# The two layers of an MLP alternate by threes: one chunk of the first layer, then one token block of the second

## The chip, the cores and the metric

The kernel runs on one core of one Trainium2 chip. The metric is the device time of one launch in microseconds, as the median of several runs. For the kernel before, the median of three runs is 957.42 us (957.02 to 958.61). Beside these stands one profiled execution. The TensorE (PE) does the matrix products and the transposes, VectorE (DVE) and ScalarE (ACT) read their results out of PSUM, GpSimd (POOL) works on SBUF alone, and SyncE (SP) starts all the transfers.

## The reference

The reference is a windowed attention followed by a two-layer MLP, in float32.

```python
# q, k, v: (batch 8, heads 8, 576, 64)
scores = scale * np.matmul(q, k.transpose(0, 1, 3, 2))
# heads 0-3: the last 32 keys; heads 4-7: every 4th of the last 128 keys
scores = np.where(masks[None, :, :, :], scores, -1000000000.0)
attn = softmax(scores)                       # written out in the original
x = (attn @ v).transpose(0, 2, 1, 3).reshape(4608, 512)
h = x @ w_in                                 # 512 -> 2048
g = np.where(h >= 1, h, np.where(h <= -1, 0.0, (h + 1) ** 2 / 4))
out = g @ w_out                              # 2048 -> 512
```

## The kernel before

**Attention.** A head is worked on in six query tiles of 96 rows, each against 128 keys. Scores go to PSUM (tag `att`, two banks), DVE adds the mask and takes the minimum for the softmax (lines 169 and 240), ACT takes the exponentials (L246), DVE and POOL normalise (L260, L263, L264), DVE transposes (L286; for the first 16 heads TensorE does, L310), TensorE multiplies with the values (L344), and `store_x` splits the result into a rounded part `xh` (ACT, L328) and a rest `xl` (DVE, L329). These are the tokens of the MLP, kept in SBUF.

**MLP.** The 4608 tokens are nine tiles of 512 (`t`), and the 2048 hidden units are sixteen blocks of 128 (`f`). A step is one pair (t, f), so there are 144 steps, f inside t. Every product is made of three in the fast float32 format: high by high, low by high, high by low.

- `layer1(t, f)`: one PSUM bank `h` (tag `h`, two banks) gets 12 matmuls of 128x512, that is four chunks `c` of the 512 inputs with three terms each (L382). Then come five operations on it, here called the chain: DVE clamps h into `y` (L396), ACT squares it (L399), DVE takes the maximum back into the bank (L401), ACT rounds it to `gh` (L402), DVE stores the rest `gl` (L405). `gh` and `gl` have two buffers each.
- `layer2(t, f)`: for each of four token blocks `m` of 128, three matmuls of 128x512 accumulate onto bank `acc0` to `acc3` (L418). After f = 15 each `acc` is copied out by ACT (L430) or DVE (L428) and stored from there (L431). So these four banks, the two of `h` and the two of `att` are the eight banks of PSUM.

**Order.** The instructions of TensorE and SP stand exactly in the order in which the program writes them; those of DVE, ACT and POOL are put in order when the program is built, by a simulated time line with priorities. The chain is raised by 60 places, the score reductions of later heads by 100. The second layer runs two steps behind the first (`lag = 2`). The work of attention hangs on slots: `run(u)` issues what is placed on slot u, and a step s has two of them, `run(2 * s)` and `run(2 * s + 1)`. From head 16 on, slots go in fours: three successive slots hold the scores of two query tiles each (the third also the split of the next head's q and k, the loads and the softmax), and every second time the fourth holds the products with the values. The three lie on slots 2s + 1 of an odd step and 2s and 2s + 1 of the even step after it, the values on slot 2s of an odd step. The DVE transposes of a head are written down with the first scores of the head after it. The last slot is in step 111; after it the steps consist of the MLP alone.

**The weights.** Each of the 32 weight tiles arrives as float64 and is turned into two tiles by ACT, DVE and POOL (L115 to L132). `behind(marks, ...)` puts that work on ACT and DVE after the chain of a given step: in step s the tile `wo` s and the tile `wi` s+3 come after the chain of step s-2.

**Start.** Half of the first layer of steps 0 and 1 (chunks 0 and 1) is done before the loop. The loop's steps 0 and 1 add chunks 2 and 3 to them. Slots 0 and 1 hold the TensorE transposes of heads 8 and 9, slot 2 their values, slots 3 and 4 the scores of heads 10 and 11.

Of the kernel before, what the change touches and what calls it, by code (L numbers as in the profile page):

```python
# [35 lines left out]
TOK = 512  # L36
NT = B * S // TOK
NF = DF // 128
NC = DM // 128
# [5 lines left out]
def body(ctx, tc, q, k, q2, k2, v, mask, eye, w_in, w_out, out):  # L45
# [23 lines left out]
    def load_pair(n):  # L69

        if 0 < n < H:
            qr, kr = borrow(f"qr{n}")[:, :S], borrow(f"kr{n}")[:, :KPAD]
        else:
            tags = ("qs", "kk") if n % 4 else ("qr", "kr")
            qr = pool.tile([128, S], F32, tag=tags[0], name=f"qr{n}")
            kr = pool.tile([128, KPAD], F32, tag=tags[1], name=f"kr{n}")
        nc.sync.dma_start(out=qr, in_=q[n // 2])
        nc.sync.dma_start(out=kr, in_=k[n // 2])
        for j in range(2):
            r = slice(64 * j, 64 * j + 64)  # L80
            heads[n + j] = dict(qs=qr[r], ks=kr[r])
# [8 lines left out]
    def load_values(n):  # L90
        if 0 < n < H:
            vt = borrow(f"vt{n}")[:, : 2 * NQ * D]
        else:
            vt = pool.tile([128, 2 * NQ * D], F32, tag="vt", name=f"vt{n}", bufs=2)
        nc.sync.dma_start(out=vt, in_=v[n // 2])
        vt = vt.rearrange("p (j t d) -> p j t d", j=2, t=NQ)
        for j in range(2):
            heads[n + j]["vt"] = vt[:, j]
# [3 lines left out]
    def fetch(f, src, name):  # L102

        raw = pool.tile([128, 2 * DM], U32, tag=f"{name}{f}", name=f"{name}_raw{f}")
        nc.sync.dma_start(out=raw, in_=src[:, f].bitcast(U32))
        raws[name, f] = raw
# [210 lines left out]
    def xtile(t):  # L317
        if t not in xt:
            xt[t] = (
                pool.tile([128, NC, TOK], F32R, tag="xh", name=f"xh{t}", bufs=3),  # L320
                pool.tile([128, NC, TOK], F32R, tag="xl", name=f"xl{t}", bufs=3),
            )
        return xt[t]
# [47 lines left out]
    gs = {}  # L371
# [3 lines left out]
    def layer1(t, f, cs=range(NC), bank=("h", 2)):  # L375
        xh, xl = xtile(t)
        if cs[0] == 0:
            hps[t, f] = ps.tile([128, TOK], F32, tag=bank[0], name=f"h{t}_{f}", bufs=bank[1])
        hp = hps[t, f]
        terms = [(w, x, c) for c in cs for w, x in ((0, xh), (1, xh), (0, xl))]  # L380
        for i, (w, x, c) in enumerate(terms):
            PE.matmul(  # L382
                out=hp,
                lhsT=wi[f][:, w, 128 * c : 128 * c + 128],
                rhs=x[:, c],
                start=c == 0 and i == 0,
                stop=c == NC - 1 and i == len(terms) - 1,
            )
        if cs[-1] < NC - 1:
            return  # L390
        del hps[t, f]
        y = pool.tile([128, TOK], F32, tag="y", name=f"y{t}_{f}")
        gh = pool.tile([128, TOK], F32R, tag="gh", name=f"gh{t}_{f}", bufs=2)
        gl = pool.tile([128, TOK], F32R, tag="gl", name=f"gl{t}_{f}", bufs=2)
        with tc.high_priority(offset=60):
            nc.vector.tensor_scalar(  # L396
                out=y, in0=hp, scalar1=-1.0, scalar2=1.0, op0=ALU.max, op1=ALU.min
            )
            nc.scalar.activation(out=y, in_=y, func=AF.Square, bias=half_t, scale=0.5)  # L399

            activated = nc.vector.tensor_tensor(out=hp, in0=hp, in1=y, op=ALU.max)  # L401
            copied = nc.scalar.copy(out=gh, in_=hp)  # L402
            if t == 0:
                last["g", f] = copied, activated
            nc.vector.tensor_tensor(out=gl, in0=hp, in1=gh.bitcast(F32), op=ALU.subtract)  # L405
        gs[t, f] = gh, gl

    acc = {}

    def layer2(t, f):  # L410
        gh, gl = gs.pop((t, f))
        for m in range(TOK // 128):
            if f == 0:
                acc[m] = ps.tile([128, DM], F32, tag=f"acc{m}", name=f"acc{t}_{m}")
            r = slice(128 * m, 128 * m + 128)
            terms = ((gh, 0), (gl, 0), (gh, 1))
            for i, (g, w) in enumerate(terms):
                PE.matmul(  # L418
                    out=acc[m],
                    lhsT=g[:, r],  # L420
                    rhs=wo[f][:, w],
                    start=f == 0 and i == 0,
                    stop=f == NF - 1 and i == len(terms) - 1,
                )
            if f == NF - 1:
                o = pool.tile([128, DM], F32, tag="m", name=f"out{t}_{m}", bufs=3)
                if m % 2:
                    nc.vector.tensor_copy(out=o, in_=acc[m])  # L428
                else:
                    nc.scalar.copy(out=o, in_=acc[m])  # L430
                nc.sync.dma_start(out=out[t * TOK + 128 * m : t * TOK + 128 * m + 128], in_=o)  # L431
# [8 lines left out]
    def after_pair(n):  # L440
        softmax(n)
        softmax(n + 1)
        if n + 4 < native:
            load_pair(n + 4)
        elif n + 4 == native:
            load(native)
        else:
            split(native)
            load(native + 1)
# [50 lines left out]
    def pair(n):  # L500
        scores_pair(n, 0, 4)
        scores_pair(n, 4, NQ)
        if n < H // 2:
            for t in range(NQ):
                exp(n, t)
                exp(n + 1, t)
            normalise(n, nc.gpsimd)
            normalise(n + 1, nc.gpsimd)
        else:
            whole(n)  # L510
            whole(n + 1)
            normalise(n, nc.gpsimd)
            normalise(n + 1, nc.vector)

    def early_transposes(n):
        with tc.high_priority(offset=150):
            transpose_pe(n)
            transpose_pe(n + 1)

    def early_values(n):  # L520
        with tc.high_priority(offset=150):
            values(n)

    def behind(marks, *blocks):

        with tc.issue_after(marks[0].ins), tc.issue_after(marks[1].ins):
            for name, f in blocks:
                weights(f, {"wi": wi, "wo": wo}[name], name)

    def marks():  # L530
        return last["act"], last["dve"]

    def run(u):
        for op in slots.pop(u, ()):
            op()

    with tc.manual_schedule(engines={mybir.EngineType.PE, mybir.EngineType.SP}):
        pair(0)
        pair(2)
        pair(4)  # L540
        pair(6)
        scored = marks()
        early_transposes(0)
        load_values(8)
        fetch(1, w_out, "wo")
        fetch(4, w_in, "wi")
        load_pair(10)
        fetch(2, w_out, "wo")
        fetch(5, w_in, "wi")
        fetch(3, w_out, "wo")  # L550
        for f in range(6, 9):
            fetch(f, w_in, "wi")
            fetch(f - 2, w_out, "wo")
        early_transposes(2)
        early_values(0)
        behind(scored, ("wi", 0), ("wi", 1))
        early_transposes(4)
        early_values(2)
        first = marks()
        early_transposes(6)  # L560
        early_values(4)
        behind(first, ("wi", 2), ("wo", 0))
        second = marks()
        layer1(0, 0, range(2))
        layer1(0, 1, range(2))
        early_values(6)
        scores_pair(H, 0, 4)
        scores_pair(H, 4, NQ)
        for f in range(9, NF):
            fetch(f, w_in, "wi")  # L570
            fetch(f - 2, w_out, "wo")
        fetch(NF - 2, w_out, "wo")
        fetch(NF - 1, w_out, "wo")
        after_pair(H)
        behind(second, ("wi", 3))
        l2 = 0
        steps = [(t, f) for t in range(NT) for f in range(NF)]
        lag = 2
        for s in range(len(steps) + lag):
            if 0 < s < NF:  # L580
                todo = [("wo", s)]
                if s + 3 < NF:
                    todo.append(("wi", s + 3))
                behind(last["g", max(s - 2, 0)], *todo)
            if s < 2:
                layer1(*steps[s], range(2, NC))
            elif s < len(steps):
                layer1(*steps[s])
            run(2 * s)
            while l2 <= s - lag and l2 < len(steps):  # L590
                layer2(*steps[l2])
                l2 += 1
            run(2 * s + 1)
        assert not slots


# [61 lines left out]
```

## Time and profile before

| | before |
|---|---|
| median of three runs | 957.42 us |
| the profiled execution's own time | 957.35 us |
| its span, first to last instruction | 955.6 us |
| mean granted TensorE clock | 0.982 |
| PE busy | 924.7 us (97%) |
| DVE busy | 732.5 us (77%) |
| ACT busy | 484.1 us (51%) |
| POOL busy | 233.9 us (24%) |

The span leaves 1.75 us of the profiled execution's time outside. Times inside the profile are counted from the span's start. A busy PE is not a PE at its peak: the matmuls overlap, each is shown with about 0.39 us, and they start about 0.23 us apart. So the distance between starts is the price of a matmul. In the groups by line, the last column is the idle time of that engine ahead of these instructions, and the releaser that ended it. DVE and ACT rows of the time line carry the same in brackets.

### The profile page before, as it was taken

How to read it: one execution, taken by the hardware profiler on the slowest of the kernel's cores; microseconds unless marked ns; L12 is line 12 of the kernel's file. 1: busy time of each engine (PE TensorE's matmuls, PEld its weight loads, DVE VectorE, ACT ScalarE, POOL GpSimd, SP SyncE). 2: the span in 40 equal slices, each digit the busy share in tenths (PEclk: the TensorE clock that was granted, in tenths of full speed). 3: DMA queues.
4: the chain of work that ended last, by engine and by line, in shares of the span. 5: the costliest groups of instructions: out<-in, count | busy, mean ns of one | idle time of the engine just before them, and what ended most of it. 6: DMA issues, size and time to landing. Idle time of an engine off the chain costs nothing.

```text
span 955.6 us, 14440 instructions
## 1 busy us (share of the span) xinstructions
PE 924.7 (97%) x4822; PEld 749.4 (78%) x4822; DVE 732.5 (77%) x2033; ACT 484.1 (51%) x1335; POOL 233.9 (24%) x150
## 2 busy tenths in 40 slices
PE   6759999999999999999999999999999999999998
PEld 6637778887878888888888888878888788888886
DVE  6777887988888889888998899888998743334333
ACT  5676875555555555555555555555555332222222
POOL 4344452222212222222222222222222100000000
PEclk9869999999999999999999999999999999999999
DMA  9961101322122223222132223222222010001001
GB/s 347 402 240 43 43 27 43 112 69 67 43 96 68 68 68 104 77 69 67 56 100 68 68 69 112 68 68 65 89 66 73 1 45 1 0 1 45 1 1 44
DMA packets 31018, 73.86 MB, mean 77 GB/s; under 512 B 3520, under 2 KB 3808, under 8 KB 30944
## 3 DMA queue, kind: packets, MB, share of 16 engines
q1 hardware_dynamic: 30944, 72.94, 23.5%
q8 instruction: 38, 0.62, 0.3%
q14 instruction: 36, 0.29, 0.1%
HBM read 63.49 MB, written 9.44 MB: 76 GB/s over the span
## 4 chain that ended last, share of the span: by engine, by line
PE 90%; DVE 4%; ACT 3%; DMA 2%; issue 1%; SPq 0%; ACTq 0%; DVEq 0%
PE h L382 40%; PE acc L418 40%; PE o L344 4%; PE s L221 4%; ACT c L246 2%; DVE c L260 1%; DMA wo_raw<-w_in 1%; PE s L198 1%; DMA kr<-k_in 1%; PE t L310 1%; PE s L195 1%; DVE pt L286 0%; ACT y L399 0%; DVE c L278 0%; DVE c L169 0%
## 5 line engine op out<-in xcount | busy, mean ns | idle before, releaser
L418 PE MATMUL acc<-wo,gh 128*128 128x512 f32 x1152 | 384.1, 395 | 0.0
L382 PE MATMUL h<-xh,wi 128*128 128x512 f32 x1152 | 363.5, 397 | 0.0
L418 PEld LDWEIGHTS acc<-wo,gh 128*128 128x128 f32 x1152 | 216.2, 188 | 48.3
L382 PEld LDWEIGHTS h<-xh,wi 128*128 128x128 f32 x1152 | 211.1, 190 | 42.3 <-issue 0.3
L382 PE MATMUL h<-xl,wi 128*128 128x512 f32 x576 | 228.3, 396 | 0.0
L418 PE MATMUL acc<-wo,gl 128*128 128x512 f32 x576 | 225.1, 391 | 0.0
L246 ACT ACTIVATE c<-c 96x128 f32<-96x128 f32 x360 | 140.5, 392 | 148.4 <-DVE c L169 148.4
L143 POOL TENSOR_TENSOR kk<-kr,kk 128x608 fp32r<-128x608 f32 x48 | 95.1, 1981 | 404.5 <-ACT kk L139 404.5
L399 ACT ACTIVATE y<-y,consts 128x512 f32<-128x512 f32 x144 | 104.2, 724 | 163.2 <-DVE y L396 156.5
L401 DVE TENSOR_TENSOR h<-h,y 128x512 f32<-128x512 f32 x144 | 100.7, 699 | 64.0 <-ACT y L399 63.1
L396 DVE TENSOR_SCALAR y<-h 128x512 f32<-128x512 f32 x144 | 97.1, 674 | 51.8 <-PE h L382 51.7
L405 DVE TENSOR_TENSOR gl<-h,gh 128x512 fp32r<-128x512 f32 x144 | 98.6, 685 | 43.4 <-ACT gh L402 42.9
L382 PEld LDWEIGHTS h<-xl,wi 128*128 128x128 f32 x576 | 109.0, 189 | 25.6
L402 ACT CAST gh<-h 128x512 fp32r<-128x512 f32 x144 | 84.8, 589 | 81.3 <-PE acc L418 55.6
L418 PEld LDWEIGHTS acc<-wo,gl 128*128 128x128 f32 x576 | 108.2, 188 | 21.1
L286 DVE STREAM_TRANSPOSE pt<-c 32x192 f32<-32x192 f32 x288 | 105.9, 368 | 3.5
L264 POOL TENSOR_TENSOR c<-c 96x768 f32<-96x768 f32 x62 | 91.3, 1475 | 63.8 <-DVE c L263 57.8
L260 DVE SCALAR_TENSOR_TENSOR c<-c 96x6 f32<-96x6 f32 x64 | 69.5, 1085 | 8.8 <-ACT c L246 6.2
L240 DVE TENSOR_TENSOR c<-s,msk 96x256 f32<-96x256 f32 (+1 forms) x168 | 61.4, 377 | 14.4 <-PE s L221 13.2
L169 DVE CUSTOM_DVE_ANT_0 c<-s,c 96x128 f32<-96x128 f32 x288 | 70.6, 281 | 1.0
L246 ACT ACTIVATION_READ_ACCUMULATOR c<-c 96x1 f32 x360 | 67.7, 188 | 0.0
L221 PEld LDWEIGHTS s<-kk,qs 128*96 128x96 f32 x288 | 45.0, 161 | 20.3 <-issue 5.9
(49 smaller groups left out, 649.8 us busy)
## 6 DMA issues: line engine op xcount, KB each, us to landing
kr<-k_in SPq DMA_DIRECT2D x56, 304.0 KB, 3.3
qr<-q_in SPq DMA_DIRECT2D x56, 288.0 KB, 2.8
vt<-v_in SPq DMA_DIRECT2D x32, 384.0 KB, 4.0
out<-out SPq DMA_DIRECT2D x36, 256.0 KB, 3.1
wi_raw<-w_in SPq DMA_DIRECT2D x16, 512.0 KB, 9.4
wo_raw<-w_in SPq DMA_DIRECT2D x16, 512.0 KB, 10.2
msk<-mask_in SPq DMA_DIRECT2D x1, 144.0 KB, 4.4
ident<-eye_in SPq DMA_DIRECT2D x1, 36.0 KB, 5.0
```

The source lines that it names most:

```text
L143: nc.gpsimd.tensor_tensor(out=kk[:, 1], in0=hd["kr"], in1=kk[:, 0].bitcast(F32), op=ALU.subtract)
L221: PE.matmul(out=sv[:, t - t0], lhsT=hd["qs"][:, t * QT : (t + 1) * QT], rhs=hd["ks"][:, :, t * QT : t * QT + 128], start=True, stop=True,)
L246: last["act"] = nc.scalar.activation(out=c[:, t], in_=c[:, t], func=AF.Exp, bias=st[:, 0, t : t + 1], scale=-1.0, accum_out=st[:, 1, t : t ...
L264: done = engine.tensor_tensor(out=c, in0=c, in1=spread(st[:, 2]), op=ALU.mult)
L286: nc.vector.transpose(out=pt[r : r + 32, :, 32 * g : 32 * g + 32], in_=c[32 * g : 32 * g + 32, :, r : r + 32],)
L382: PE.matmul(out=hp, lhsT=wi[f][:, w, 128 * c : 128 * c + 128], rhs=x[:, c], start=c == 0 and i == 0, stop=c == NC - 1 and i == len(terms) - 1,
L396: nc.vector.tensor_scalar(out=y, in0=hp, scalar1=-1.0, scalar2=1.0, op0=ALU.max, op1=ALU.min)
L399: nc.scalar.activation(out=y, in_=y, func=AF.Square, bias=half_t, scale=0.5)
L401: activated = nc.vector.tensor_tensor(out=hp, in0=hp, in1=y, op=ALU.max)
L402: copied = nc.scalar.copy(out=gh, in_=hp)
L405: nc.vector.tensor_tensor(out=gl, in0=hp, in1=gh.bitcast(F32), op=ALU.subtract)
L418: PE.matmul(out=acc[m], lhsT=g[:, r], rhs=wo[f][:, w], start=f == 0 and i == 0, stop=f == NF - 1 and i == len(terms) - 1,)
```

## The change

The order in which TensorE gets the matmuls of a step changes, and with it the place of the two slots.

- Before, a step s was: all 12 products of `layer1(s)`, `run(2s)`, all 12 of `layer2(s - 2)`, `run(2s + 1)`.
- After, it is: `run(2s)`, then for i = 0 to 3 three products of chunk i of `layer1(s)` and three of token block i of `layer2(s - 2)`; behind i = 1 stands `run(2s + 1)`.

The chain of step s is still issued behind chunk 3, which now stands three matmuls ahead of the end of the step. The number and the shape of all instructions stay the same, as do the buffers.

```diff
-    def layer2(t, f):
-        gh, gl = gs.pop((t, f))
-        for m in range(TOK // 128):
+    def layer2(t, f, ms=range(TOK // 128)):
+        gh, gl = gs[t, f]
+        for m in ms:
...
-        l2 = 0
         steps = [(t, f) for t in range(NT) for f in range(NF)]
         lag = 2
         for s in range(len(steps) + lag):
...
-            if s < 2:
-                layer1(*steps[s], range(2, NC))
-            elif s < len(steps):
-                layer1(*steps[s])
             run(2 * s)
-            while l2 <= s - lag and l2 < len(steps):
-                layer2(*steps[l2])
-                l2 += 1
-            run(2 * s + 1)
+            for i in range(NC):
+
+                if s < len(steps) and (s >= 2 or i >= 2):
+                    layer1(*steps[s], range(i, i + 1))
+                if s >= lag:
+                    layer2(*steps[s - lag], range(i, i + 1))
+                if i == 1:
+                    run(2 * s + 1)
```

## The prediction, made before the changed kernel was run

> **What bounds the kernel now.** I read the page's first part, then its costliest groups, then the busy time by stretches, and last the time line in three places: the part after attention has ended, the middle, and the start.
>
> ```profile
> span 955.6 us, 14440 instructions
> PE 924.7 (97%) x4822; PEld 749.4 (78%) x4822; DVE 732.5 (77%) x2033; ACT 484.1 (51%) x1335; POOL 233.9 (24%) x150
> ...
> L418 PE MATMUL acc<-wo,gh 128*128 128x512 f32 x1152 | 384.1, 395 | 0.0
> ...
> L402 ACT CAST gh<-h 128x512 fp32r<-128x512 f32 x144 | 84.8, 589 | 81.3 <-PE acc L418 55.6
> ```
> ```profile
> 40.00:75.00 35.00, 23.05 (x149) 17.68 (x147) 23.37 (x75) 24.96 (x77) 14.46 (x11) 0.71 0.64 252
> ...
> 372.00:474.00 102.00, 101.95 (x533) 82.27 (x532) 91.07 (x262) 55.39 (x163) 27.59 (x16) 1.00 0.25 74
> ...
> 755.00:943.00 188.00, 188.00 (x835) 153.08 (x834) 76.05 (x116) 47.27 (x75) 0.00 (x0) 1.00 0.03 12
> ```
>
> The columns of the stretches are their length, the busy time of PE, its weight loads, DVE, ACT and POOL, then PE's granted clock. PE is busy 101.95 of 102 us in the middle and 188.00 of 188 in the part after attention. So from about 75 us on there is no hole in PE that another order could fill; only 40 to 75 us has holes (23.05 of 35 busy, clock 0.71). DVE is second in the middle: 91.07 of 102 us. The change can therefore work in four ways: by the distance between matmul starts, by a hole that it opens, by the start, and by the end. The 55.6 us that ACT waits in front of `gh` for the second layer are not on PE's path.
>
> **The distance between starts.** The part after attention shows one step undisturbed.
>
> ```profile
> 851.48 0.62 PE L382 MATMUL h<-xh,wi 128*128 128x512 f32 x2
> ...
> 852.18 0.63 PE L382 MATMUL h<-xh,wi 128*128 128x512 f32 x2
> ...
> 854.04 0.39 PE L382 MATMUL h<-xl,wi 128*128 128x512 f32 x1
> ...
> 854.27 0.39 PE L418 MATMUL acc<-wo,gh 128*128 128x512 f32 x1
> ...
> 854.47 0.69 DVE L396 TENSOR_SCALAR y<-h 128x512 f32<-128x512 f32 x1 [1.48 <-PE h L382]
> ...
> 854.97 0.19 PEld L418 LDWEIGHTS acc<-wo,gl 128*128 128x128 f32 x1
> ...
> 855.26 0.72 ACT L399 ACTIVATE y<-y,consts 128x512 f32<-128x512 f32 x1 [2.99 <-DVE y L396]
> ...
> 856.01 0.70 DVE L401 TENSOR_TENSOR h<-h,y 128x512 f32<-128x512 f32 x1 [0.85 <-ACT y L399]
> ...
> 857.01 0.62 PE L382 MATMUL h<-xh,wi 128*128 128x512 f32 x2
> 857.21 0.59 ACT L402 CAST gh<-h 128x512 fp32r<-128x512 f32 x1 [1.23 <-PE acc L418]
> ...
> 857.83 0.69 DVE L405 TENSOR_TENSOR gl<-h,gh 128x512 fp32r<-128x512 f32 x1 [1.11 <-ACT gh L402]
> ```
>
> A step runs from 851.48 to 857.01: 5.53 us, of which the first layer has 854.27 - 851.48 = 2.79 and the second 2.74, that is 0.2325 and 0.228 a matmul. The switch from the first layer to the second costs no more than any other neighbour: 854.27 - 854.04 = 0.23. The change turns two switches a step into eight. The first three after a switch took 0.70 in each layer (852.18 - 851.48, and to 854.97, where the loads for block 1's second product start with its first product), of 0.6975 and 0.685 on the mean of their layers. From both sides: if all triples came to the second layer's mean, a step is 8 x 0.685 = 5.48, -0.05 x 144 = -7 us; if all came to the first layer's 0.6975, 5.58, +7 us. I take -0.01 a step, since the last distance of each triple becomes a switch (0.23) where the first layer had 0.2325: -1.5 us.
>
> **The chain, and what it loses.** In the time line above, the last product of a first layer starts at 854.04 and `gl` ends at 858.52, 4.48 later. In it `gh` waits for the second layer of two steps before (the bracket: 1.23 until PE's acc). After the change that layer ends three matmuls after the first one does, so `gh` follows line 401 at once (856.71), `gl` ends 0.62 + 0.69 later plus a start of 0.03, at 858.05: 4.01. This gain has no taker here, PE being full. The price stands at the other end. Bank `h` is written again two steps later, when `gl` has read it. Before, from the last product of a step to the first that reuses its bank are 36 matmuls in between, 37 distances, 8.5 us; after, 3 + 24 = 27 in between, 28 distances of 0.23, 6.44 us. Against 4.01 that leaves 2.4 us after attention has ended: free. The second layer's use of `gl` is three matmuls later still.
>
> In the middle DVE serves attention too:
>
> ```profile
> 374.32 0.39 PE L382 MATMUL h<-xl,wi 128*128 128x512 f32 x1
> ...
> 375.77 0.65 DVE L396 TENSOR_SCALAR y<-h 128x512 f32<-128x512 f32 x1
> ...
> 377.26 0.70 DVE L401 TENSOR_TENSOR h<-h,y 128x512 f32<-128x512 f32 x1 [0.25 <-ACT y L399]
> 377.32 0.40 PE L221 MATMUL s<-kk,qs 128*96 128x256 f32 x2
> ...
> 377.87 2.27 DVE L286 STREAM_TRANSPOSE pt<-c 32x192 f32<-32x192 f32 x6
> 378.05 0.59 ACT L402 CAST gh<-h 128x512 fp32r<-128x512 f32 x1 [0.35 <-DVE h L401]
> ...
> 380.52 0.68 DVE L428 COPY out<-acc 128x512 f32<-128x512 f32 x1
> ...
> 381.12 0.68 DVE L405 TENSOR_TENSOR gl<-h,gh 128x512 fp32r<-128x512 f32 x1
> ...
> 383.57 0.62 PE L382 MATMUL h<-xh,wi 128*128 128x512 f32 x2
> ...
> 386.44 1.43 PE L344 MATMUL o<-pt,vt 128*64 128x96 f32 x24
> ```
>
> Here 374.32 to 383.57 is 9.25 us: 37 distances of 0.23, and 0.74 for the three score slots in between, 0.25 each. `gl` ends at 381.80, 7.48 after the last product: 1.77 to spare. After the change nine matmuls (2.07) and one score slot (0.25) fall out of this window: 6.93 remain. The same order on DVE would be 0.55 late. But this is a step with an output copy (380.52, 0.68), and six transposes (2.27) stand in front of `gl`. DVE's order comes from a simulated time line in which `gh` waits for the second layer; I read their place as a filling of that wait. In the new program the wait is gone, and the gap there is one `gh` (0.59). Taking off the copy and half the transposes gives 7.48 - 0.6 - 1.1 = 5.8 of 6.93. In every second pair of steps the values (1.43) widen the window. I take no wait in the middle, but 0.6 us in all for the steps up to 150 us, where ACT and DVE also make the weights. Bounds: 0, and the 0.55 of this row in each of the 48 pairs of steps 16 to 111, 26 us.
>
> **The start.**
>
> ```profile
> 53.48 1.22 PE L310 MATMUL t<-ident,c 96*128 96x96 f32 x6 [5.83 <-POOL c L264]
> ...
> 57.28 0.63 PE L382 MATMUL h<-xl,wi 128*128 128x512 f32 x1
> 57.71 1.05 PE L382 MATMUL h<-xh,wi 128*128 128x512 f32 x2
> ...
> 59.12 1.90 PE L344 MATMUL o<-pt,vt 128*64 128x96 f32 x24
> 63.95 0.74 PE L198 MATMUL s<-kr,qr 64*96 64x128 f32 x2 [2.93 <-DVE xl L329]
> 67.22 1.99 PE L198 MATMUL s<-kr,qr 64*96 64x128 f32 x14 [2.53 <-DVE xl L329]
> 69.14 1.22 PE L382 MATMUL h<-xh,wi 128*128 128x512 f32 x2
> ```
> ```profile
> 61.77 1.76 DVE L126 SCALAR_TENSOR_TENSOR wi_m<-wi_m,wi_raw 128x512 uint32<-128x512 uint32 x1
> 63.45 0.67 DVE L329 TENSOR_TENSOR xl<-o,xh 128x288 fp32r<-128x288 f32 x2
> ...
> 64.65 1.62 DVE L126 SCALAR_TENSOR_TENSOR wo_m<-wo_m,wo_raw 128x512 uint32<-128x512 uint32 x1
> ...
> 66.79 0.28 DVE L329 TENSOR_TENSOR xl<-o,xh 128x128 fp32r<-128x128 f32 x1
> ```
>
> Slots 0 and 1 now stand ahead of the six products that finish step 0. These had run before the hole of 5.83 that POOL ends; now they come after the transposes, in the place of step 1's six, and step 1's six come behind slots 2 and 3. So six products leave the hole and lie on the path: 6 x 0.23 = 1.4 us, or 6 x 0.43 (57.71 - 57.28, the clock then being low) = 2.6. Against this: step 0's chain ends later, and the weights that stand behind it with it. The two waits of 2.93 and 2.53 are for `xl`, which stood on DVE behind such weight work (61.77, 64.65). If `xl` comes first, up to 5.46 of them go. I take half of that, -2.7, with +1.4: -1.3 us. Bounds: 1.4 - 5.5 = -4.1, and +2.6. What is late next are those weights: step 0's products now end where step 1's did, before 59.12, and the first step that uses weights behind them, step 3, comes a step of 5.53 after the one that begins at 69.14: over 15 us for them, 0.
>
> **The end.** After the last first layer there were 24 matmuls until its `gl` is used, now 15. From its last product to the first second-layer product with `gl` are 17 distances, 3.9 us, against 4.01 and a start: +0.2 us (bounds 0 and 0.6). Four copies of `acc` that came within one second layer are now spread over a step: 0, DVE and ACT having room there. SP's loads of a slot now stand between the stores of blocks 1 and 2: 0, a head being loaded more than a step ahead.
>
> **The sum.** The profiled execution took 957.35 us, 1.75 beside its span; the median is 957.42. 957.35 - 1.5 + 0.6 - 1.3 + 0.2 = 955.35.
>
> **The rivals.**
> (a) Bank `h` comes free too late. The place is `gl` behind transposes and scores on DVE, the price what the chain exceeds 6.9 us by, once in two steps, since PE waits in order. For it: the row of 7.48, and DVE at 91 of 102. Against: the gone wait of `gh`. At 0.55 in half the pairs (the others have the values) 13 us, in all 26: 968 to 981. It decides from a chain of 6.9 us on.
> (b) The switches are cheap and the start gains: -7 - 2.7 + 1.4: 949. For it: 0.685 in the second layer, which changes banks each third matmul.
> (c) It does nothing to PE's stream and the start loses its six products: 957.35 + 1.4 + 0.2 = 959. For it: no hole in PE from 75 us on.
> (d) The change of banks makes PE's clock fall. The second layer shows it does not, at a bank every three matmuls and clock 1.00 in the stretch 755 to 943. If it did in a tenth of the 144 steps, at 0.43 instead of 0.23 that is 14.4 x 5.53 x 0.87 = 69 us: 1026. The Trainium skill, "TensorE: Matmul & The Clock Gate", section "A second HAM failure mode: psum-queue depth-cycling", speaks for (d): it says that a kernel whose matmuls cycled through PSUM banks left PE idle for moments often enough that its clock swung between half and full. By that rule the time would be that of (d); this trace disagrees with it so far, with 188.00 of 188 us busy at clock 1.00.
>
> **How the numbers follow.** The forecast has 0.50, (a) 0.20, (b) 0.15, (c) 0.12, (d) 0.03. About 0.2%, 1.9 us, is what a measurement of this kernel tells from no change. The forecast lies 2.0 below and its own range is 950 to 960: 0.25 faster, 0.17 same, 0.08 slower. (a) gives 0.02 same and 0.18 slower, (b) 0.15 faster, (c) 0.08 same and 0.04 slower, (d) 0.03 slower. Together 0.40, 0.27, 0.33. The range goes from 947, the sum with the low ends of the switches and the start (957.35 - 7 - 4.1 + 0.2 + 0.6), to 968, the near end of (a); beyond lie half of (a), (d) and little below, some 0.17.
>
> **What will show it.** Distances: a step after attention of 5.52 us; 5.48 speaks for (b). Chain: the wait of `gh` for acc near 0 instead of 55.6 us, and PE's products of line 382 without idle time released by DVE's `gl`; with such idle time of over 5 us, (a). Start: the two waits of the scores for `xl` together below 5.46 us. The prediction is wrong if PE's busy share in the middle falls, or if the distance of starts leaves 0.228 to 0.2325.

## The result: 59 us slower

| | before | after |
|---|---|---|
| median of four runs each | 957.22 us (956.64 to 958.61) | 1016.28 us (1013.75 to 1016.87) |
| ratio to before | | 1.061 (1.0588 to 1.0631) |
| profiled execution, span | 955.6 us | 1014.3 us |
| mean granted TensorE clock | 0.982 | 0.969 |

The forecast was 955.4 us, between 947 and 968. It was wrong, in sign and in size. The page of the kernel after, its first part and the costliest groups that answer to those shown:

```profile
PE 943.2 (93%) x4822; PEld 757.0 (75%) x4822; DVE 730.2 (72%) x2033; ACT 490.4 (48%) x1335; POOL 216.8 (21%) x150
...
L382 PE MATMUL h<-xh,wi 128*128 128x512 f32 x1152 | 370.6, 403 | 1.1 <-DVE gl L405 1.1
...
L402 ACT CAST gh<-h 128x512 fp32r<-128x512 f32 x144 | 84.6, 587 | 56.7 <-DVE h L401 49.0
L221 PE MATMUL s<-kk,qs 128*96 128x256 f32 x288 | 58.4, 284 | 37.1 <-DVE xl L329 36.4
```

The last row is new: the scores (L221) stood 37.1 us, and `xl` on DVE ended 36.4 of it. The products of L382 waited 1.1 us for `gl`, so bank `h` is not the cause. The stretches, columns as in the prediction, first the steps 16 to 111 of before, then the same 96 steps of after and a stretch behind its attention:

```profile
163.50:768.50 605.00, 604.23 (x3160) 488.85 (x3159) 535.87 (x1542) 322.22 (x944) 160.12 (x93) 1.00 0.24 72
```
```profile
167.20:825.40 658.20, 620.44 (x3160) 496.84 (x3159) 534.88 (x1538) 326.89 (x944) 142.77 (x93) 0.98 0.21 66
...
830.00:1000.00 170.00, 170.00 (x734) 137.28 (x733) 66.44 (x96) 42.23 (x65) 0.00 (x0) 1.00 0.04 13
```

The same 3160 matmuls took 658.2 us instead of 605.0: 53.2 of the 58.7 us by which the span grew. PE stood idle 658.20 - 620.44 = 37.8 us of it, against 0.8 before, and its clock fell to 0.98. After attention it is as full as before.

One of the places shows how. This is the time line of after in step 27; of PE only the values and scores and, behind them, some products are shown.

```profile
237.21 1.49 POOL L143 TENSOR_TENSOR kk<-kr,kk 128x608 fp32r<-128x608 f32 x1 [8.13 <-PE h L382]
...
237.59 1.73 DVE L140 TENSOR_TENSOR qs<-qr,qs 64x576 fp32r<-64x576 f32 x1
237.77 1.43 PE L344 MATMUL o<-pt,vt 128*64 128x96 f32 x24
...
239.35 0.69 DVE L396 TENSOR_SCALAR y<-h 128x512 f32<-128x512 f32 x1
...
240.07 0.16 DVE L260 SCALAR_TENSOR_TENSOR c<-c 96x6 f32<-96x6 f32 x1
...
240.76 0.84 ACT L328 CAST xh<-o 128x192 fp32r<-128x192 f32 x2
...
241.50 0.91 DVE L329 TENSOR_TENSOR xl<-o,xh 128x192 fp32r<-128x192 f32 x2
...
242.33 1.89 DVE L286 STREAM_TRANSPOSE pt<-c 32x192 f32<-32x192 f32 x5
244.24 0.69 DVE L405 TENSOR_TENSOR gl<-h,gh 128x512 fp32r<-128x512 f32 x1
244.94 0.37 DVE L286 STREAM_TRANSPOSE pt<-c 32x192 f32<-32x192 f32 x1
245.34 0.55 DVE L329 TENSOR_TENSOR xl<-o,xh 128x96 fp32r<-128x96 f32 x2
245.81 0.45 PE L221 MATMUL s<-kk,qs 128*96 128x256 f32 x2 [3.63 <-DVE xl L329]
...
248.92 0.63 PE L418 MATMUL acc<-wo,gh 128*128 128x512 f32 x1
...
249.35 0.63 PE L418 MATMUL acc<-wo,gl 128*128 128x512 f32 x1
```

And before at the same place:

```profile
233.29 0.76 DVE L140 TENSOR_TENSOR qs<-qr,qs 64x576 fp32r<-64x576 f32 x1
...
233.37 2.02 POOL L143 TENSOR_TENSOR kk<-kr,kk 128x608 fp32r<-128x608 f32 x1 [8.23 <-ACT kk L139]
...
234.10 1.30 DVE L260 SCALAR_TENSOR_TENSOR c<-c 96x6 f32<-96x6 f32 x1
...
234.12 1.43 PE L344 MATMUL o<-pt,vt 128*64 128x96 f32 x24
...
235.09 0.50 ACT L328 CAST xh<-o 128x192 fp32r<-128x192 f32 x1 [1.02 <-PE o L344]
...
235.55 0.65 DVE L396 TENSOR_SCALAR y<-h 128x512 f32<-128x512 f32 x1
...
236.12 0.50 DVE L329 TENSOR_TENSOR xl<-o,xh 128x192 fp32r<-128x192 f32 x1
...
237.66 0.49 DVE L329 TENSOR_TENSOR xl<-o,xh 128x192 fp32r<-128x192 f32 x1
...
238.35 0.28 DVE L329 TENSOR_TENSOR xl<-o,xh 128x96 fp32r<-128x96 f32 x1
238.66 1.90 DVE L286 STREAM_TRANSPOSE pt<-c 32x192 f32<-32x192 f32 x5
238.77 0.45 PE L221 MATMUL s<-kk,qs 128*96 128x256 f32 x2 [0.27 <-DVE xl L329]
```

The products with the values lie in the two `att` banks, and so do the scores of the next slot, half a step later. That slot needs the bank which the third piece of `xl` reads last. Before, from the values' start to the scores' start are 238.77 - 234.12 = 4.65 us, and the scores already waited 0.27: there was no room. After, they are 8.04. Two things on DVE are new, and one on ACT. The subtraction of line 140 takes 1.73 us instead of 0.76, since POOL's line 143 started first, and `y` stands right behind it. By itself this does not make DVE later than before: there line 260 ran beside POOL's line 143 and took 1.30 us, against 0.16 now, and `y` started 1.43 us behind the values, now 1.58. But ACT's order is another. Before, ACT made the first piece of `xh` ahead of the square of `y`, 0.97 us behind the start of the values; now it makes it behind that square, 2.99 us behind them, and stands idle 1.88 us for `y` ahead of the square. So a late `y` now makes `xh` late, and `xl` with it. And DVE's new order puts six transposes (1.89 + 0.37) and `gl` ahead of the small pieces of `xl`, where before the third piece stood ahead of all but one transpose. A little behind the wait the matmuls start 0.43 apart (248.92, 249.35) instead of 0.23.

Worked out from the starts of the first-layer products, the 58.7 us lie so: +4.0 up to step 16, +52.9 from there to step 112, +1.4 to the last step, +0.4 behind it. In the middle, 11 score waits, two in sixteen steps, and seven short waits of L382 make about 38 us more than before had. (From start to start the 11 are 2.9 to 3.8 us long; the profile's idle time, which counts a matmul as longer than the distance to the next, has 2.77 to 3.67.) Some fifty matmuls at half clock, in stretches of mostly 3.4 us, make about 10, and the longer distances between matmuls (below) 96 x 0.046 = 4.4.

### The profile page after: what moved, and what is told of

Read it like the earlier page. It is cut to its first block, busy times and chain, and to the rows that moved or that the text cites. A ratio compares the mean times of both kernels' runs of the same rounds, so it can differ in the third digit from the quotient of the medians.

```text
span 1014.3 us, 14443 instructions
## 1 busy us (share of the span) xinstructions
PE 943.2 (93%) x4822; PEld 757.0 (75%) x4822; DVE 730.2 (72%) x2033; ACT 490.4 (48%) x1335; POOL 216.8 (21%) x150
## 4 chain that ended last, share of the span: by engine, by line
PE 47%; DVE 31%; ACT 13%; issue 5%; POOL 4%; DMA 0%; ACTq 0%; POOLq 0%; DVEq 0%
PE h L382 22%; PE acc L418 21%; DVE pt L286 8%; ACT c L246 6%; DVE qs L140 5%; DVE gl L405 4%; POOL c L264 4%; ACT y L399 3%; DVE y L396 3%; DVE c L169 2%; DVE c L240 2%; DVE xl L329 2%; PE s L221 2%; ACT gh L402 2%; DVE h L401 1%
## 5 line engine op out<-in xcount | busy, mean ns | idle before, releaser
L418 PE MATMUL acc<-wo,gh 128*128 128x512 f32 x1152 | 457.3, 398 | 0.0
L382 PE MATMUL h<-xh,wi 128*128 128x512 f32 x1152 | 370.6, 403 | 1.1 <-DVE gl L405 1.1
L418 PEld LDWEIGHTS acc<-wo,gh 128*128 128x128 f32 x1152 | 219.4, 190 | 51.3
L382 PEld LDWEIGHTS h<-xh,wi 128*128 128x128 f32 x1152 | 206.6, 191 | 44.1 <-DVE gl L405 2.7
L418 PE MATMUL acc<-wo,gl 128*128 128x512 f32 x576 | 230.8, 401 | 0.1
L382 PE MATMUL h<-xl,wi 128*128 128x512 f32 x576 | 230.0, 399 | 0.0
L143 POOL TENSOR_TENSOR kk<-kr,kk 128x608 fp32r<-128x608 f32 x48 | 77.1, 1605 | 444.0 <-ACT kk L139 387.1
L401 DVE TENSOR_TENSOR h<-h,y 128x512 f32<-128x512 f32 x144 | 100.5, 698 | 53.2 <-ACT y L399 51.9
L382 PEld LDWEIGHTS h<-xl,wi 128*128 128x128 f32 x576 | 110.2, 191 | 25.5
L221 PE MATMUL s<-kk,qs 128*96 128x256 f32 x288 | 58.4, 284 | 37.1 <-DVE xl L329 36.4
L221 PEld LDWEIGHTS s<-kk,qs 128*96 128x96 f32 x288 | 45.9, 164 | 58.9 <-issue 42.3
```

Source lines behind the costliest of these rows:

```text
L221: PE.matmul(out=sv[:, t - t0], lhsT=hd["qs"][:, t * QT : (t + 1) * QT], rhs=hd["ks"][:, :, t * QT : t * QT + 128], start=True, stop=True,)
L382: PE.matmul(out=hp, lhsT=wi[f][:, w, 128 * c : 128 * c + 128], rhs=x[:, c], start=c == 0 and i == 0, stop=c == NC - 1 and i == len(terms) - 1,
L418: PE.matmul(out=acc[m], lhsT=g[:, r], rhs=wo[f][:, w], start=f == 0 and i == 0, stop=f == NF - 1 and i == len(terms) - 1,)
```

## The experiments

My theory (A in most of the expectations below): the loss is this wait, made of the new things on DVE, with the half clock as its consequence. The rivals: alternating as such costs it (distances, clock, or bank `h`), or the new slots as such.

**Slots alone.** The slots stand where the change puts them, without the alternation.

```diff
             run(2 * s)
-            for i in range(NC): ...
+            if s < len(steps):
+                layer1(*steps[s], range(2 if s < 2 else 0, NC))
+            run(2 * s + 1)
+            if s >= lag:
+                layer2(*steps[s - lag])
```

> The slots stand where the change puts them (slot 2s ahead of the step, slot 2s+1 in its middle), but the layers do not alternate: twelve of the first, the slot, twelve of the second. Theory A (the order of DVE: the last pieces of xl stand behind five transposes and a gl, the att bank comes free late, and the scores behind the values hold TensorE up): in this program only one to four transposes stand in front of these pieces, so the waits of the scores shrink from 40 us in all to under 5, no half clock in the middle, step after attention 5.53 us; 957 to 964 us. Theory B (the new place of the slots is the cost by itself, whatever stands between them): 1000 us or more, with the score waits still at about 40. Theory C (alternation itself makes TensorE slower): 957 to 960.

Measured: 958.91 us, ratio 1.0016 (1.0006 to 1.0026). The scores of L221 wait for no `xl`, line 140 takes 0.759 us on the mean and a step after attention 5.527. So the new slots alone do not do it. What they cost is at the start: step 16 begins 6.4 us later than before, and the 96 steps from there give 4.8 us of that back.

**Alternation, slots half a step later.** The threes stay, `run(2s)` moves behind i = 1 and `run(2s + 1)` to the end of the step.

```diff
-            run(2 * s)
             for i in range(NC):
                 ...
                 if i == 1:
-                    run(2 * s + 1)
+                    run(2 * s)
+            run(2 * s + 1)
```

> The layers alternate by threes as in the change, but the slots stand half a step later: slot 2s behind the second pair of triples, slot 2s+1 at the end of the step. Theory A: here the last pieces of xl stand behind no or three transposes, so score waits of 5 to 12 us in all instead of 40; the step after attention stays at 5.57; 968 to 978 us. Theory B: about 965, of which 7 for the switches. Theory C (alternation costs most of the 59 us, by late chains and banks): 1005 or more.

Measured: 958.19 us, 1.0007 (0.9997 to 1.0016). The waits of the scores are gone altogether, where theory A had left 5 to 12 us of them, and the time lies below every range given beforehand. So the alternation alone does not do it either: the loss needs the alternation and the slots at these places together. That speaks for something that both have a hand in, as they have in the order and the timing of DVE and ACT.

**The transposes behind `xl`.** The kernel after, each DVE transpose bound to follow the DVE operation noted last, which for the transposes written down behind the values is the last `xl` (lines move by one: `xl` is L330, the transposes L287).

```diff
+                with tc.issue_after(last["dve"].ins):
-                nc.vector.transpose(...)
+                    nc.vector.transpose(...)
+                    nc.vector.transpose(...)
```

> The changed kernel, with one order added on DVE: the transposes of a head stand behind the last piece of xl written down before them. Theory A: two to five transposes (up to 2.2 us) leave each of the 11 long score waits, 3.7 becomes about 1.5 and 3.0 about 1; score waits about 15 us instead of 40; no half clock in the middle (10 us less); 975 to 985 us. If DVE is late for another cause (its whole backlog, not this order), the waits stay above 30 us and the time above 1005.

Measured: 982.96 us, 1.0269 (1.0253 to 1.0284): 33 us of the 59 gone, as theory A expected. All idle time ahead of L221 comes to 13.5 us instead of 37.1, and the middle has no half clock. The time line at the same place:

```profile
236.78 1.73 DVE L140 TENSOR_TENSOR qs<-qr,qs 64x576 fp32r<-64x576 f32 x1
...
242.09 0.54 DVE L330 TENSOR_TENSOR xl<-o,xh 128x96 fp32r<-128x96 f32 x2
242.54 0.74 DVE L287 STREAM_TRANSPOSE pt<-c 32x192 f32<-32x192 f32 x2
242.55 0.45 PE L221 MATMUL s<-kk,qs 128*96 128x256 f32 x2 [1.17 <-DVE xl L330]
```

The transposes stand behind; line 140 still takes 1.73 us, and the wait is 1.17 instead of 3.63.

**Alternating by sixes.** Two chunks, then two blocks; the slots as in the change.

```diff
-            for i in range(NC):
+            for i in range(0, NC, 2):
-                    layer1(*steps[s], range(i, i + 1))
+                    layer1(*steps[s], range(i, i + 2))
                 ... (layer2 likewise)
-                if i == 1:
+                if i == 0:
                     run(2 * s + 1)
```

> The layers alternate by sixes, two chunks and then two blocks; the slots as in the change. Theory A: six transposes and a gl stand ahead of the last pieces of xl, as many as in the change, so the score waits stay at 35 us or more, with the half clock: 1005 to 1015 us. For the switches alone (four instead of eight a step) the step after attention comes to 5.55 us, 3.3 us less in all. Theory C (alternation by threes is itself the cost): about 985, half way back.

Measured: 984.74 us, 1.0279 (1.0264 to 1.0295), some 20 us under what I expected. The number is the 985 of theory C, but not its reason: 21.1 us are again waits of the scores for `xl`, four of them with half clock behind them, and a step after attention takes 5.533 us. The same place shows why the waits are shorter:

```profile
232.59 0.76 DVE L140 TENSOR_TENSOR qs<-qr,qs 64x576 fp32r<-64x576 f32 x1
...
232.98 1.71 POOL L143 TENSOR_TENSOR kk<-kr,kk 128x608 fp32r<-128x608 f32 x1 [8.34 <-ACT kk L139]
...
236.59 2.28 DVE L286 STREAM_TRANSPOSE pt<-c 32x192 f32<-32x192 f32 x6 [0.15 <-POOL c L264]
...
239.51 0.54 DVE L329 TENSOR_TENSOR xl<-o,xh 128x96 fp32r<-128x96 f32 x2
239.97 0.45 PE L221 MATMUL s<-kk,qs 128*96 128x256 f32 x2 [1.86 <-DVE xl L329]
```

Here the six transposes stand ahead, but DVE's line 140 starts ahead of POOL and takes 0.76. So this run has the one cause and the run before it the other: 1.86 and 1.17 us of wait, together 3.03 against 3.63 with both. It is no clean test of the one cause, since its order on TensorE is another too.

**Line 140 off DVE.** In both runs POOL computes line 140; in the first the transposes are also bound behind `xl`, in the second they are left to the order that comes out.

```diff
-        nc.vector.tensor_tensor(   # line 140: qs = qr - qs
+        nc.gpsimd.tensor_tensor(
```

> As xl_first (the changed kernel with the transposes behind the last xl), and the subtraction of q's rest of line 140 runs on POOL instead of DVE. In the changed kernel that DVE operation runs beside POOL's subtraction of line 143 and takes 1.33 us on average instead of 0.76, just ahead of y, so that y, its square on ACT, and behind it xh and xl come late; by_sixes, where it takes 0.78, has 23 us of score waits instead of 40 although six transposes stand ahead of xl. Theory A2 (two causes that add: the transposes and this collision): with both gone, score waits under 4 us, what is left is the start and 0.046 us a step for the switches; 963 to 970 us. If the collision is no cause: as xl_first, 980 to 985.

Measured: 961.0 us, 1.0039 (1.0024 to 1.0055). All waits of L221 for `xl` together are 0.4 us.

> The change as it is, with line 140 (the low part of q, DVE beside POOL's line 143) moved to POOL; the transposes stay ahead of the xl pieces. With the transposes put behind, this edit took 22 us off (983.0 to 961.0). Theory A, the two causes add: a long wait falls from 3.6 to about 2.6 us (line 140 took 1.73 us instead of 0.76 ahead of it), and part of the half clock behind the waits goes; 990 to 1000, the scores' waits for xl at 20 to 28 us instead of 36.4. Rival B, the transposes hide it (xl waits for them whenever line 140 ends): the waits stay at 33 us or more and the time at 1010 or above. Rival C, line 140 is nearly all of it: below 975, waits under 10 us.

Measured: 963.8 us, 1.0071 (1.0054 to 1.0088). By its number that is rival C, but the time line does not bear out C's reason:

```profile
237.57 0.32 DVE L329 TENSOR_TENSOR xl<-o,xh 128x96 fp32r<-128x96 f32 x1
237.80 0.36 DVE L286 STREAM_TRANSPOSE pt<-c 32x192 f32<-32x192 f32 x1
238.10 0.28 DVE L329 TENSOR_TENSOR xl<-o,xh 128x96 fp32r<-128x96 f32 x1
238.28 0.40 PE L221 MATMUL s<-kk,qs 128*96 128x256 f32 x2
```

Taking one instruction from DVE made its order anew, and the transposes moved behind `xl` by themselves (between the small pieces stands one instead of six ahead of them). So this edit removed both causes at once and cannot weigh them; binding the transposes and alternating by sixes, which each leave one of them, can do so roughly.

The same place in step 27 of these kernels, in us from the start of the values:

| | `y` starts (DVE) | first `xh` starts (ACT) | the `xl` that the scores need starts | wait of the scores |
|---|---|---|---|---|
| before | 1.43 | 0.97 | 4.23 | 0.27 |
| after | 1.58 | 2.99 | 7.57 | 3.63 |
| transposes behind `xl` | 1.57 | 2.98 | 5.12 | 1.17 |
| by sixes | -0.31 | 1.11 | 5.81 | 1.86 |
| line 140 on POOL, transposes behind `xl` | -0.59 | 0.97 | 3.52 | 0 |
| line 140 on POOL | -0.59 | 0.97 | 3.53 | 0 |

Moving line 140 let `y` start 2.16 us earlier, and `xh` with it. It did not end the collision on DVE: POOL's line 143 now meets line 260, which takes 1.38 us there, but behind `y`. Of the 2.16 us, about 0.97 (1.73 against 0.76) is what the collision adds to line 140, and the rest is that line 140 stood ahead of `y` at all. No run parts these two: none leaves line 140 at its place in the kernel after without the collision.

**By sixes, slots half a step later.** I hoped to join the cheaper distances of the sixes to the later slots.

```diff
             for i in range(0, NC, 2):
                 ...
                 if i == 0:
-                    run(2 * s + 1)
+                    run(2 * s)
+            run(2 * s + 1)
```

> The layers alternate by sixes, with the slots half a step later as in slots_later. By the step after attention (5.573 by threes, 5.533 by sixes, 5.527 without alternation), 0.04 x 144 = 5.8 us less than slots_later, whose middle and start were 2 us ahead of the kernel before: 952 to 955 us, faster than before. If the cost by threes is not one of the step but of something that sixes bring too: 958.

Measured: 975.73 us, 1.02 (1.0184 to 1.0215), against my expectation of a gain. The chain of waits that the prediction had called rival (a) appears here:

```profile
PEld h L382 <- DVE gl L405: 14.5, 31, 2.3
...
PE h L382 <- DVE gl L405: 6.3, 14, 1.9
```

The columns are total, number and longest wait in us. PE's loads and products of L382 wait for `gl`: bank `h` comes free too late. (The two rows overlap in time and do not add; they leave part of the 18.5 us lost open.)

**Slots half a step early, from step 15 on, no alternation.** This keeps the start of before and takes the middle of the first experiment; the edit is shown against the kernel before.

```diff
+            early = s >= 15
+            if early:
+                run(2 * s)
             layer1(...)
-            run(2 * s)
+            run(2 * s + early)
             layer2(...)
-            run(2 * s + 1)
+            if not early:
+                run(2 * s + 1)
```

> The kernel before, without alternation; from step 15 on the slots stand half a step earlier (slot 2s ahead of the step, 2s+1 between the layers), as in slots_only; up to step 14 as before. slots_only lost 6.4 us up to step 16 and won 4.8 from there to step 112. If the middle's gain is its own: 952 to 954.5 us, faster than before. If it was only the loss of the start made up for (work that had been pushed back): 957 to 958.

Measured: 952.92 us, 0.9955 (0.9942 to 0.9967): the fastest of all, and 0.45% faster than the kernel before, as expected if the middle's gain is its own. The 96 middle steps:

```profile
163.50:764.00 600.50, 600.50 (x3160) 490.10 (x3159) 498.54 (x1534) 336.20 (x940) 142.45 (x93) 1.00 0.24 72
```

600.5 us instead of 605.0. Half of that is seen at one kind of place: the distance from the last product ahead of a score slot to the slot was 0.255 on the mean of 93 slots behind the second layer before, and is 0.230 in the 93 behind the first layer now, 2.3 us. The other half I did not take apart.

## Why the prediction was wrong

**The step that failed is "I take no wait in the middle".** It followed one consumer of DVE's work, bank `h` behind `gl`, and for that it was right: 1.1 us of waits at L382 in after, against 0.6 forecast for the chain and 26 as the bound. For the middle it never asked who waits for the other results of DVE once its order is made anew. What came there was 36 us of waits of the scores (L221) for `xl`, and about 10 us of half clock behind them. The prediction said that DVE's order comes from a simulated time line, and it took half the transposes as falling away from in front of `gl`; it did not ask in front of what they would go instead, nor what becomes of ACT's order, which is computed in the same way. The scores' wait of 0.27 for `xl` in before was the row to read: an edge of the `att` banks without slack, met twice in sixteen steps at the pieces that are cut over two token tiles. Its bound of 26 us was for another edge.

**Rival (a)** had the right kind (a bank comes free too late, behind transposes on DVE) at the wrong bank. Its own place came to more than 2 us only by sixes with later slots.

**The half clock** came, but not by rival (d). PE's banks change eight times a step in the stretch after attention, and the clock there is 1.00 with 170.00 of 170 us busy. So the rule that the prediction weighed from the Trainium skill ("TensorE: Matmul & The Clock Gate", section "A second HAM failure mode: psum-queue depth-cycling") is not borne out here either. The half clock follows the waits. By sixes it followed shorter ones; the time line and a stretch of that kernel:

```profile
345.65 0.45 PE L221 MATMUL s<-kk,qs 128*96 128x256 f32 x2 [1.92 <-DVE xl L329]
```
```profile
346.00:350.00 4.00, 4.00 (x13) 3.15 (x13) 1.62 (x6) 1.60 (x5) 0.00 (x0) 0.63 0.00 0
```

The Trainium skill, "TensorE: Matmul & The Clock Gate", section "What's actually happening", says that the clock drops to half after an idle window of about 3.4 us, and that this window runs free of the program. The length of the stretches at half clock agrees; a wait of 1.92 us was enough here, which is shorter than the window.

Not every wait was followed by half clock: 7 of the 11 in the kernel after were, and a second wait of 1.92 us by sixes, at 451.3, was not. The records of the clock show why. Behind 100 us, all its falls to half clock in each of these two traces lie whole multiples of 3.413 us apart. Cut along that grid, each stretch of the middle at full clock that held 1.86 us or more of idle PE was followed by half clock, and none that held 1.82 or less. The 1.92 us ahead of 345.65 fell into one stretch; the 2.86 us ahead of 275.7 in the kernel after fell into two, 1.82 and 1.04, and cost no clock. (Ahead of step 16, where PE also had the smaller matmuls of L198, a stretch with 1.72 was enough.)

**The distances** were sized wrong: -1.5 us taken, +6.6 came. A step after attention:

```profile
900.68 0.62 PE L382 MATMUL h<-xh,wi 128*128 128x512 f32 x2
...
901.37 0.39 PE L418 MATMUL acc<-wo,gh 128*128 128x512 f32 x1
...
902.07 0.62 PE L382 MATMUL h<-xh,wi 128*128 128x512 f32 x2
...
906.25 0.62 PE L382 MATMUL h<-xh,wi 128*128 128x512 f32 x2
```

906.25 - 900.68 = 5.57 us, where 5.52 was forecast. The triple of the second layer, 0.685 in before on its layer's mean, takes 902.07 - 901.37 = 0.70 now; that of the first, 0.69. On 24 steps the distance is 5.573 by threes, 5.533 by sixes and 5.527 without alternation. The prediction's upper bound, all triples like the first layer's (5.58, +7 us), was the answer; that the first three after a switch took 0.70 in both layers stood in its own rows, and I took the mean instead.

**The start** was to give 1.3 us, and at the start of step 3, with the same work behind it, the kernel after is 1.35 us ahead (76.34 against 77.69). That is partly luck. The hole that POOL ends grew from 5.83 to 7.48, about the 1.4 for the six products; the two score waits for `xl` fell from 5.46 to 4.09, by 1.37 where 2.7 was taken; the rest is that the half clock ended at 69.8 instead of 73.8, which no term of the sum held. From there to step 16 the kernel after fell back to 4.0 us behind. About 4.9 of these 5.3 are seen: a third score wait for `xl` of 0.70 at 94.10, 1.72 of idle time ahead of the scores at 122.75 (the profile names no releaser; the last pieces of `xl` end on DVE about then) and some 1.4 by the half clock behind it, a wait of 0.46 at 152.07, and 0.6 by the distances.

**The chain** of `gh` went as forecast: its 55.6 us of waiting for the second layer are gone, and it now waits 49.0 us for DVE's line 401. As the prediction said, PE had no use for that. **The end** cost 0.4 instead of 0.2.

## What to carry to other kernels

Where an engine's order is computed, a change on another engine changes it too: list every result of that engine which the bound engine waits for, with its slack before, and take the smallest, not the one that the change is about. A wait of a few tenths in the trace of before is not small change but the mark of an edge with no slack. And a fix that takes an instruction away must be read in the new order before it is credited to that instruction.

## What the hardware showed that I had not expected

Lines 140 and 260 on DVE (both with two operands in SBUF) and POOL's line 143, their means in before and then in after:

```profile
L143 POOL TENSOR_TENSOR kk<-kr,kk 128x608 fp32r<-128x608 f32 x48 | 95.1, 1981 | 404.5 <-ACT kk L139 404.5
...
L260 DVE SCALAR_TENSOR_TENSOR c<-c 96x6 f32<-96x6 f32 x64 | 69.5, 1085 | 8.8 <-ACT c L246 6.2
...
L140 DVE TENSOR_TENSOR qs<-qr,qs 64x576 fp32r<-64x576 f32 x48 | 36.3, 755 | 1.5
```
```profile
L143 POOL TENSOR_TENSOR kk<-kr,kk 128x608 fp32r<-128x608 f32 x48 | 77.1, 1605 | 444.0 <-ACT kk L139 387.1 <-PE h L382 56.9
L140 DVE TENSOR_TENSOR qs<-qr,qs 64x576 fp32r<-64x576 f32 x48 | 63.8, 1328 | 2.5 <-ACT qs L138 1.2
...
L260 DVE SCALAR_TENSOR_TENSOR c<-c 96x6 f32<-96x6 f32 x64 | 19.5, 305 | 5.5 <-ACT c L246 3.9
```

Which of the two pays depends on which starts first. In step 27 of before DVE started 0.08 us ahead and POOL took 2.02; in after POOL started 0.38 ahead, and DVE ended at 239.32, 0.62 after POOL's end at 238.70. The Trainium skill, "SBUF — State Buffer", section "Who interferes with whom", says that such a DVE instruction and a GpSimd one that reads SBUF take a shared port as a lock, the order of issue deciding who blocks; the trace agrees, with 0.76 against 1.73 us for one instruction. A shift of half a microsecond between two engines thus put 0.97 us on line 140. It did not make DVE pay more in all: line 260, which in before started beside line 143 and ended with it (234.10 + 1.30 = 235.40, POOL at 235.39), had paid more, and the two lines of DVE together fell from 105.8 to 83.3 us. What counted was which instruction paid, and who stood behind it.
